# A convolution stem's gradients: paired sums, joins in SBUF, and four more leaves by three products

## The chip, the cores and the metric

The kernel runs on one core of one Trainium2 chip. The metric is the device time in microseconds of one execution; the profile is that of one such execution, and its span runs from the first to the last instruction. TensorE (PE) multiplies matrices into PSUM; VectorE (DVE) and ScalarE (ACT) read PSUM and SBUF; GpSimd (POOL) does small fills; SyncE (SP) issues the transfers.

## What is computed

```python
L = (T - K) // 2 + 1                                   # B, T, D, K = 2, 16000, 256, 31; L = 7985
h = sum over i of einsum('blc,cd->bld', x[:, i:i + 2 * L:2, :], w[i])
mu = mean over l of h;  var = mean over l of (h - mu) ** 2
h = (h - mu) / sqrt(var + 1e-5) * gn_gamma + gn_beta
out = gelu(h)                                          # tanh form
returns out and the gradients of x, w, gn_gamma, gn_beta for grad_out
```

Everything large is bf16. There are three products of the size of the convolution: the forward one, the gradient of x and the gradient of w.

## The kernel before, in words

Each of the three convolutions is cut by three levels of a fast scheme that takes three half-size products in place of four: a sum or difference of operands, called branch or leaf B, and the products A and C. At the outer two levels this gives nine combinations of branch (`br`) and leaf (`lf`). At the innermost level a leaf is done either by four products (`f_leaf`, `g_leaf`, `w_leaf`) or by three: a first part on differenced weights (`f_three_b`, `g_three_b`, `w_pairs`), whose result ACT copies within PSUM with the needed signs, and a second part on summed data added on top (`f_three_ac`, `g_three_ac`, `w_single`). PSUM is a ring of four tiles of 128 x 1024 fp32.

The stages follow each other on PE:

- **Forward** (matmuls at L655): two batches, four chunks each, three branches each. `f_sums` (L609 to 640, its `tt` at L620) makes the summed data: `second` the leaves' operands, `third` the third level's. The leaves of the branches in `FO` are done by three products through `f_outer`, which computes the first parts of A and C into one PSUM tile and copies them with both signs to SBUF (L725); `f_seed` (L735, L739, L792) then adds the B leaf, `RB` and those copies into PSUM ahead of the second parts. `f_evac` (L770, L783) copies the results to SBUF with sums for the mean, and squares them for the variance into a junk tile `JK`.
- **Gelu** (`gelu_unit`, L1014 to L1040) of batch 0 runs beside the forward part of batch 1, that of batch 1 beside the first chunks of the input gradient. A unit is one half of the channels, 128 x 1024: load, Identity and Square on ACT, L1018 on DVE, two sigmoids on ACT (L1020, L1022), L1024 and five products or sums at L1028 on DVE, then two accumulated sums (L1038 on ACT, L1040 on DVE). Its tiles come in rings: three or two sets of h, y and s, and two or one of the scratch tiles y2 and z.
- **Input gradient** (matmuls at L1217): `e_load` and `e_comp` form the gradient of the normalised value, `e_spread` (L1155) lays it out, `g_sums` (L1181) makes the sums. `plain` serves the first three chunks of batch 0, `split` (all leaves by three products) the other five; the results are joined by `g_join` (L1259) and stored. `d2_piece` (L1410) makes differences of the output gradient for the next stage. `w2_outer` makes the differenced weights that `split` needs ahead of the fourth chunk.
- **Weight gradient** (matmuls at L1500): nine combinations in turn. `x_tile` loads x and, in some, adds (`w_add`, L1466); `pair_x` (L1560), `pair_d` (L1568) and `leaf_d` (L1638) make operands. `NODES` lists the ten of eighteen leaves done by three products. The partial sums are fp32 in SBUF; DVE adds them to PSUM (`ve` at L735, `w_both` at L1592) and, at the end of a leaf, writes the output (`w_emit`, L1529).

The order is not the order of the program text. Every operation is recorded by `Plan.add` with a planned duration and the tiles it reads and writes; `Plan.listing` then puts each engine's operations into a fixed list by due times, which the matmuls set, shifted by kind in the table `lead`. The engines run these lists in order. GpSimd's and SP's lists are made in the same way, and all large transfers are issued by SP.

## Time and profile before

| | |
|---|---|
| three runs | 1184.16, 1186.21, 1187.15 us; median 1186.21 |
| the profiled execution | 1185.89 us, span 1184.1 us, mean granted TensorE clock 0.986 |
| PE, weight loads, DVE, ACT busy | 1120.7, 751.0, 1043.5, 595.9 us |
| forward, first to last matmul | 7.9 to 429.5 us |
| input gradient | 429.5 to 862.6 us |
| weight gradient | 862.7 to 1179.0 us |
| transfers | 255 MB, mean 215 GB/s |

Busy time is the time in which at least one instruction of the engine runs; matmuls overlap each other, so their mean duration is longer than their spacing, and neighbouring DVE and ACT instructions overlap a little. In a row of a group stand the line, the engine, the operation with tiles and shapes and the count; then busy time and mean ns of one; then idle time of the engine just ahead of them and what ended it. In a row of the timeline stand start and duration. A window's row gives stretch, length, busy time and count of PE, weight loads, DVE, ACT and POOL, the granted clock, the share of the transfer engines and GB/s.

### The profile page before, as it was taken

The page shows a single profiled execution, that of the slowest core. Times are in us where ns is not written, and L with a number is a line of the kernel's source. Part 1 is how long each engine was busy: PE and PEld are TensorE (multiplying, and loading weights), DVE is VectorE, ACT ScalarE, POOL GpSimd, SP SyncE. Part 2 cuts the span into 40 slices and gives each one's busy share as a digit, 9 for nine tenths or more (in the row PEclk, how much of TensorE's full clock was granted, in tenths as well). Part 3 has the DMA queues.
Part 4 walks back from the last instruction along what each step waited for, and adds up shares of the span by engine and source line. Part 5 has one row for each costly group of instructions (what it writes and reads, how often), then busy time and mean ns, then how long its engine had stood idle before and what let it go on. Part 6 is the DMA issues. An engine that isn't in the chain of part 4 may idle for free.

```text
span 1184.1 us, 19217 instructions
## 1 busy us (share of the span) xinstructions
PE 1120.7 (95%) x7615; PEld 751.0 (63%) x7668; DVE 1043.5 (88%) x1410; ACT 595.9 (50%) x919; POOL 38.7 (3%) x67
## 2 busy tenths in 40 slices
PE   3999999999999969989999899999999999989998
PEld 3888899867677954434444344444478766656785
DVE  6997887899999978989899898889999999689994
ACT  1253444778686488676867777664522202111200
POOL 0000000000000000020000120000000000000000
PEclk7999999999999989999999999999999999999999
DMA  8358658878794798877744999889898717996783
GB/s 213 52 133 154 135 146 179 215 146 207 170 208 124 276 253 270 247 223 196 209 135 126 317 338 300 230 257 296 286 290 295 225 78 240 329 338 204 243 239 99
DMA packets 348334, 255.16 MB, mean 215 GB/s; under 512 B 187734, under 2 KB 328916, under 8 KB 341972
## 3 DMA queue, kind: packets, MB, share of 16 engines
q1 hardware_dynamic: 348052, 253.93, 75.9%
q8 instruction: 60, 0.98, 0.3%
q14 instruction: 30, 0.25, 0.1%
q0 software_dynamic: 192, 0.00, 0.0%
HBM read 118.95 MB, written 89.62 MB: 176 GB/s over the span
## 4 chain that ended last, share of the span: by engine, by line
PE 73%; DVE 10%; DMA 7%; ACT 5%; issue 3%; SPq 1%; POOL 1%; DVEq 0%; POOLq 0%; ACTq 0%; another core or an unknown queue 0%
PE ps L655 34%; PE ps L1500 20%; PE ps L1217 19%; DVE arena L1466 2%; DMA arena<-dnd 2%; DMA d2d<-arena 2%; DVE arena L1410 1%; DMA arena<-in_x_dram 1%; DVE arena L1259 1%; DMA arena<-hd 1%; SPq L480 1%; POOL arena L1146 1%; DVE arena L1181 1%; DMA arena<-d2d 1%; DVE arena L1568 1%
## 5 line engine op out<-in xcount | busy, mean ns | idle before, releaser
L1217 PE MATMUL ps<-arena 128*128 128x512 bf16 (+1 forms) x1834 | 404.5, 380 | 28.9 <-DVE arena L1181 9.0
L655 PE MATMUL ps<-arena 128*128 128x256 bf16 (+4 forms) x3460 | 406.6, 281 | 22.8 <-DVE arena L610 8.7
L655 PEld LDWEIGHTS <-arena 128*128 128x128 bf16 x3460 | 338.4, 99 | 90.8 <-DVE arena L610 8.8
L1217 PEld LDWEIGHTS <-arena 128*128 128x128 bf16 x1872 | 184.3, 99 | 248.8 <-issue 28.7
L1500 PE MATMUL ps<-arena 128*128 128x256 bf16 (+1 forms) x2321 | 309.8, 295 | 6.5 <-DVE arena L1560 4.9
L1500 PEld LDWEIGHTS <-arena 128*128 128x128 bf16 x2336 | 228.3, 98 | 88.0 <-DVE arena L1560 5.7
L750 ACT ACTIVATE arena<-ps 128x1024 bf16<-128x1024 f32 (+1 forms) x129 | 130.8, 1020 | 216.8 <-PE ps L1500 94.5
L620 DVE TENSOR_TENSOR arena<-arena 128x1088 bf16<-128x1088 bf16 (+3 forms) x211 | 174.7, 868 | 18.7 <-PE ps L655 18.1
L1028 DVE TENSOR_TENSOR arena<-arena 128x1024 bf16<-128x1024 bf16 x160 | 107.7, 686 | 10.6 <-ACT arena L1020 7.0
L1181 DVE TENSOR_TENSOR arena<-arena 128x516 bf16<-128x516 bf16 (+3 forms) x212 | 98.2, 495 | 5.3 <-PE ps L1217 2.9
L1466 DVE TENSOR_TENSOR arena<-arena 128x4096 bf16<-128x4096 bf16 x38 | 86.0, 2284 | 3.2 <-PE ps L1500 1.7
L1244 ACT ACTIVATE ps<-ps 128x512 f32<-128x512 f32 x108 | 62.3, 583 | 38.7 <-PE ps L1217 38.7
L1410 DVE TENSOR_TENSOR arena<-arena 128x768 bf16<-128x768 bf16 (+3 forms) x112 | 66.4, 638 | 10.4 <-DMA d2d<-arena 5.7
L770 ACT ACTIVATE arena<-ps 128x512 bf16<-128x512 f32 (+1 forms) x64 | 37.1, 583 | 56.0 <-PE ps L655 55.9
L1259 DVE TENSOR_TENSOR arena<-arena 128x1024 bf16<-128x1024 bf16 x80 | 54.8, 686 | 7.1 <-ACT arena L750 6.8
L1584 ACT COPY ps<-ps 128x256 f32<-128x256 f32 x54 | 19.4, 358 | 76.7 <-PE ps L1500 75.5
L1259 DVE TENSOR_TENSOR arena<-ps,arena 128x1024 bf16<-128x1024 f32 x44 | 53.7, 1220 | 3.4 <-PE ps L1217 3.3
L610 DVE TENSOR_TENSOR arena<-arena 128x2048 bf16<-128x2048 bf16 (+1 forms) x55 | 53.6, 1005 | 0.0
L725 ACT ACTIVATE arena<-ps 128x512 bf16<-128x512 f32 x56 | 29.1, 601 | 46.9 <-PE ps L655 41.7
L1018 DVE SCALAR_TENSOR_TENSOR arena<-arena 128x1024 bf16<-128x1024 bf16 x32 | 39.0, 1221 | 13.1 <-ACT arena L1016 13.0
L1568 DVE TENSOR_TENSOR arena<-arena 128x1024 bf16<-128x1024 bf16 x76 | 48.5, 685 | 1.6 <-DMA arena<-d2d 1.6
L1638 DVE TENSOR_TENSOR arena<-arena 128x2304 bf16<-128x2304 bf16 x36 | 47.7, 1351 | 2.1 <-DMA arena<-d2d 2.1
(77 smaller groups left out, 683.8 us busy)
## 6 DMA issues: line engine op xcount, KB each, us to landing
arena<-in_x_dram SPq DMA_DIRECT2D x40, 1024.0 KB, 9.5
arena<-d2d SPq DMA_DIRECT2D x16, 1216.0 KB, 13.4
out_dram<-arena SPq DMA_DIRECT2D x35, 512.0 KB, 5.6
d2d<-arena SPq DMA_DIRECT2D x30, 384.0 KB, 7.3
arena<-dnd SPq DMA_DIRECT2D x10, 960.0 KB, 5.9
vl<-arena SPq DMA_DIRECT2D x36, 256.0 KB, 3.7
arena<-vl SPq DMA_DIRECT2D x9, 1024.0 KB, 7.6
hd<-arena SPq DMA_DIRECT2D x8, 1024.0 KB, 5.0
```

Source lines behind the costliest of these rows:

```text
L620: lambda: nc.vector.tensor_tensor(out=o, in0=a, in1=b, op=ALU.add))
L655: yield nc.tensor.matmul(ps[:, dh, cs], lhsT=wt, rhs=mv, start=s0, stop=False, skip_group_check=True)
L750: lambda: nc.scalar.activation(out=out, in_=ps, func=ACT.Copy, scale=scale))
L1028: add("DVE", dve(1024), [o], [a, b_], lambda: V.tensor_tensor(out=o, in0=a, in1=b_, op=op))
L1181: lambda: nc.vector.tensor_tensor(out=o, in0=a, in1=b, op=ALU.add))
L1217: yield nc.tensor.matmul(ps[:, e, 0:wide], lhsT=lt, rhs=mv, start=s0, stop=False, skip_group_check=True)
L1244: lambda: nc.scalar.activation(out=ps[:, 1], in_=ps[:, 0], func=ACT.Copy, scale=-1.0))
L1259: add("DVE", dve(1024, rate), [o], [a, b], lambda: nc.vector.tensor_tensor(out=o, in0=a, in1=b, op=op))
L1410: lambda: nc.vector.tensor_tensor(out=out, in0=a, in1=b_, op=ALU.subtract))
L1466: add("DVE", dve(4096), [o], [a, b], lambda: nc.vector.tensor_tensor(out=o, in0=a, in1=b, op=ALU.add))
L1500: yield nc.tensor.matmul(ps[:, s, c0:c1], lhsT=lt, rhs=mv, start=s0, stop=False, skip_group_check=True)
L1568: add("DVE", dve(1024), [d4[:, j]], [d], lambda j=j, o=o, st_=st_: nc.vector.tensor_tensor(out=d4[:, j], in0=d[:, o:o + 3 * st_ + 1:st_, : ...
```

## The change

- Two helpers make access patterns: `cross` reads the two halves of a pair in reverse order, with the second one an element later (a negative step), and `fan` repeats a view twice at a given step (zero or negative too). With them `f_sums`, `g_sums`, `d2_piece` and `pair_d` write both halves of a pair by one instruction in place of two.
- `gelu_unit` works on both channel halves: tiles of 128 x 2048, two sets of h, y and s, one of y2 and z, one of the gradient and output tiles. For batch 1 the six set tiles lie at 94208 to 118784, where `w2_outer` writes later.
- Forward: `f_outer` and the seeding of PSUM in its branches go. `split` gives each leaf its own PSUM tile, does both parts in it, copies the B leaf to `TX` and forms `TP`, its sum or difference with `RB`, in SBUF; `f_evac` copies a leaf to SBUF and joins it there with `TP`. `FV` takes the place of `FO` and adds branch B of chunks 0 to 2 of batch 1.
- Input gradient: `split` makes both joined tiles at once (`VP`), with one `VX` in place of three `VT`, and joins branch B's pair at once.
- Weight gradient: fourteen of eighteen leaves by three products. `w_both` and the seeds in PSUM go: the shared part of a combination is kept in SBUF (`PM`), each finished leaf is copied by ACT and summed in bf16 in SBUF by `w_sum`. `pc_d`, a buffer in DRAM, becomes bf16.
- The table `lead` has new numbers and finer stages.

```diff
+    def cross(v, d):
+        ap = [list(x) for x in v.ap]
+        s, n = ap[d]
+        assert n == 2
+        ap[d] = [1 - s, 2]
+        return bass.AP(tensor=v.tensor, offset=v.offset + s, ap=ap)
+
+    def fan(v, d, s):
+        ap = [list(x) for x in v.ap]
+        ap.insert(d, [s, 2])
+        return bass.AP(tensor=v.tensor, offset=v.offset, ap=ap)
...
+    U = [sb(o, 2, F) for o in (138240, 142592, REG + 14336)]
...
-                tt(E1[:, 0], xt[:, 0, 3], xt[:, 1, 0])
-                tt(E1[:, 1, 0:F - 1], xt[:, 1, 3, 0:F - 1], xt[:, 0, 0, 1:F])
+                tt(E1[:, :, 0:F - 1], xt[:, :, 3, 0:F - 1], cross(xt[:, :, 0, 0:F - 1], 1))
...
-            tt(u[0], o[:, 0], o[:, 1])
-            tt(u[1][:, 0:F - 1], o[:, 1, 0:F - 1], o[:, 0, 1:F])
+            tt(u[:, :, 0:F - 1], o[:, :, 0:F - 1], cross(o[:, :, 0:F - 1], 1))
...
-                tt(lc[:, 0], E1[:, 0], E0[:, 1])
-                tt(lc[:, 1, 0:F - 1], E1[:, 1, 0:F - 1], E0[:, 0, 1:F])
+                tt(lc[:, :, 0:F - 1], E1[:, :, 0:F - 1], cross(E0[:, :, 0:F - 1], 1))
...
-    def f_outer(pt, br, ops, co, we, wd, ts):
...
-            keep(RB[:, 0 if lf == A else 1], flat2(ps))
+            keep(RB[:, 0 if lf == A else 1], flat2(ps), 1.0 if lf == A else -1.0)
+            if t is not None and lf == C_:
+                f_join(RB, RB, fan(t, 1, 0), ALU.add)
...
+        if t is not None:
+            op = ALU.add if lf == A else ALU.subtract
+            v = t[:, 0 if lf == A else 1].rearrange("p (d e f) -> p d e f", d=2, e=2)
+            o = hs[:, :, :, k, 0:wd]
+            f_join(o, o, v[:, :, :, 0:wd], op)
...
+    def f_join(o, a, b, op):
+        add("DVE", dve(o.free_size()), [o], [a, b], lambda: nc.vector.tensor_tensor(out=o, in0=a, in1=b, op=op))
...
-        if outer and br != B_:
-            for lf, j in ((C_, 1), (A, 0)):
-                t = ts[lf].rearrange("p d f -> p (d f)")
-                add("DVE", dve(1024), [t], [RB[:, j], t], lambda t=t, j=j: nc.vector.tensor_tensor(
-                    out=t, in0=RB[:, j], in1=t, op=ALU.add if br == A else ALU.subtract))
...
-    FO = {(0, c, br) for c in range(NCK) for br in ORDER if c or br != B_} | {(1, 3, br) for br in FLAST}
+    FV = {(0, c, br) for c in range(NCK) for br in ORDER if c or br != B_} | {(1, 3, br) for br in ORDER} | {(1, c, B_) for c in range(NCK)}
...
+        def split(b, c, br, sums, co, we, wo):
+            ops, third, second = sums
+            x = free.pop(0)
+            u = {B_: slot(3 - b)}
+            third(B_, u[B_])
+            f_three_b(ring[x], br, B_, ops[B_], co, we)
+            second(A)
+            step()
+            i = {A: free.pop(0)}
+            f_three_b(ring[i[A]], br, A, ops[A], co, we)
+            u[A] = slot(3 - b)
+            third(A, u[A])
+            f_three_ac(ring[x], br, B_, u[B_], co, we, wo)
+            second(C_)
+            keep(TX, flat2(ring[x]))
+            free.append(x)
+            step()
+            if br != B_:
+                f_join(TP, fan(TX, 1, 0), RB, ALU.add if br == A else ALU.subtract)
+            i[C_] = free.pop(0)
+            f_three_b(ring[i[C_]], br, C_, ops[C_], co, we)
+            u[C_] = slot(3 - b)
+            third(C_, u[C_])
+
+            def last(lf):
+                f_three_ac(ring[i[lf]], br, lf, u[lf], co, we, wo)
+                f_evac(b, c, br, lf, ring[i[lf]], TX if br == B_ else TP)
+                free.append(i[lf])
+            last(A)
+            rest.append(lambda: last(C_))
...
-    def gelu_batch(b, base, nset, nscr, ngt, noo, base0, pace):
...
+    def gelu_batch(b, areas, nset, nscr, ngt, noo, base0, pace):
...
+        hs_, ys_, ss_ = (take(nset, 2, 4, HM) for _ in range(3))
+        y2s, zs = (take(nscr, 2, 4, HM) for _ in range(2))
+        gts = take(ngt, 4, 2, XM)
+        oos = take(noo, 8, D) if noo else [None]
...
+        add("DVE", dve(2048, 1), [z], [y2, y],
...
+        add("ACT", act(2048), [s], [z],
...
-                tt(sc[:, :, 1, 0, 0:n], et[:, :, 3, 0, 0:n], et[:, :, 0, 1, 0:n])
-                tt(sc[:, :, 1, 1, 0:n - 1], et[:, :, 3, 1, 0:n - 1], et[:, :, 0, 0, 1:n])
+                tt(sc[:, :, 1, :, 0:n], et[:, :, 3, :, 0:n], cross(et[:, :, 0, :, 0:n], 2))
...
-            tt(u[:, 0, :, 0:n], e[:, :, 0, 0:n], e[:, :, 1, 0:n])
-            tt(u[:, 1, :, 0:n - 1], e[:, :, 1, 0:n - 1], e[:, :, 0, 1:n])
+            tt(u.rearrange("p j d f -> p d j f")[:, :, :, 0:n], e[:, :, :, 0:n], cross(e[:, :, :, 0:n], 2))
...
-                g_join(ts[C_], vx, GRB[:, pr, 1], ALU.subtract if br == A else ALU.add, 2)
-                g_join(vx, vx, GRB[:, pr, 0], ALU.add if br == A else ALU.subtract, 2)
+                ts = {A: VP[:, 0], C_: VP[:, 1]}
+                g_join(VP, fan(VX, 1, 0), GRB[:, pr], ALU.add if br == A else ALU.subtract, 2)
...
+                if br == B_:
+                    keep(GRB[:, pr, j], ps[:], -1.0 if lf == C_ else 1.0)
+                    if lf == C_:
+                        g_join(GRB[:, pr], GRB[:, pr], fan(VX, 1, 0), ALU.subtract, 2)
...
+        sub(t[:, :, 0:n1, :], fan(d0(2 * b1 + 1, n1), 1, -2 * D), fan(d0(2 * b1, n1), 1, 0), [t[:, :, 0:n1, :]], [dt])
...
+            sub(t2[:, k % 2, :, 0:g, :], fan(r1(1), 1, -2 * step * D), fan(r1(0), 1, 0), [t2[:, k % 2]], [v])
...
-    NODES = {(0, A), (0, C_), (1, A), (1, C_), (3, A), (4, A), (6, A), (7, A), (7, C_), (8, C_)}
...
+    NODES = {(n, lf) for n in range(9) for lf in (A, C_)} - {(1, C_), (3, C_), (5, C_), (6, C_)}
...
+    def w_sum(o, a, b):
+        add("DVE", dve(1024), [o], [a, b], lambda: nc.vector.tensor_tensor(out=o, in0=a, in1=b, op=ALU.add))
...
+        last = i1 != A and i2 != B_
+        o = (PE_[0] if n in (2, 5, 6) else w_wo() if last else PB[r3, h] if i2 == B_ else PS[r2, r3, h])
+        keep(o, flat2(ps))
+        if m is not None:
+            w_sum(o, o, m)
+        if n == 2:
+            for k in range(2):
+                w_sum(PS[k, r3, h], PS[k, r3, h], o)
...
+            w_sum(o, o, PB[r3, h])
+            w = o if i1 == C_ else w_wo()
+            w_sum(w, o, PS[r2, r3, h])
+            w_out(w, h, int(i1 == C_), r2, r3)
...
-        for j, o in ((0, o0), (1, o1)):
-            st_ = abs(o0 - o1)
-            add("DVE", dve(1024), [d4[:, j]], [d], lambda j=j, o=o, st_=st_: nc.vector.tensor_tensor(
-                out=d4[:, j], in0=d[:, o:o + 3 * st_ + 1:st_, :], in1=d[:, om:om + 3 * st_ + 1:st_, :], op=ALU.subtract))
+        s = abs(o0 - o1)
+        add("DVE", dve(2048), [d4], [d], lambda: nc.vector.tensor_tensor(
+            out=d4, in0=fan(d[:, o0:o0 + 3 * s + 1:s, :], 1, (o1 - o0) * D), in1=fan(d[:, om:om + 3 * s + 1:s, :], 1, 0), op=ALU.subtract))
...
-    def w_both(ps, t):
...
-                        if seeded:
-                            ve(t, flat2(X[h]), p2[r3, h], ALU.add)
...
+                if pa or pc:
+                    keep(PM[h], flat2(X[h]))
+                if not pa:
+                    keep(flat2(Y[h]), flat2(X[h]))
...
-    RINGS = ((3, 2, 2, 2), (2, 1, 1, 0))
+    RINGS = ((((REG, REG + 41216),), 2, 1, 1, 1), (((94208, 118784), (GREG, GREG + 20992)), 2, 1, 1, 0))
```

More of the change, by code (lines that the diff above doesn't have):

```diff
@@ new lines, in __init__ @@
+            "F1z keep split": -70.0,
+            "F1z load f_evac": -1.5,
+            "F1z tt f_sums": -56.5,
+            "F1z tt second": -16.0,
+            "F1z tt third": -8.5,
+            "F1z turn x_load": -3.5,
+            "F1z w_sub f_again": 22.0,
+            "F1z zero f_evac": -48.5,
+            "F1z zero x_load": -75.0,
+            "G0 cp e_spread": -65.0,
+            "G0 e_comp conv_stem_kernel": 2.0,
+            "G0 g_join last": -0.5,
+            "G0 g_mm g_leaf": -11.5,
@@ new lines, in __init__ @@
+            "G1 zero e_comp": -117.0,
+            "G1 zero e_spread": -14.0,
+            "G1z g_join last": -4.0,
+            "G1z g_join split": 11.0,
+            "G1z g_mm g_three_ac": -285.0,
+            "G1z g_mm g_three_b": 1.5,
+            "G1z g_three_b split": -99.0,
+            "G1z keep last": -46.5,
+            "G1z keep split": -33.5,
+            "G1z load g_store": -43.0,
+            "G1z tt first": -32.0,
+            "G1z tt second": -118.5,
+            "G1z tt third": -40.0,
@@ L189, in __init__ @@
+            "Wz turn out0_late": 24.0,
+            "Wz w_add weight_grad": 2.5,
+            "Wz w_mm w_pairs": -14.5,
+            "Wz w_mm w_single": -136.5,
+            "Wz w_pairs weight_grad": -27.0,
+            "Wz w_sum w_done": -23.5,
         }
@@ L623, in f_sums @@
         else:
[L624 removed]
+            s = S
             E0, E1 = s[:, :, 0], s[:, :, 1]
```

733 lines of the change are left out of this document (348 added, 385 removed).

## The prediction

> **What bounds the kernel now.** I read the page first: busy shares, the forty slices, the chain that ended last.
>
> ```profile
> span 1184.1 us, 19217 instructions
> PE 1120.7 (95%) x7615; PEld 751.0 (63%) x7668; DVE 1043.5 (88%) x1410; ACT 595.9 (50%) x919; POOL 38.7 (3%) x67
> PE 73%; DVE 10%; DMA 7%; ACT 5%; issue 3%; SPq 1%; POOL 1%; DVEq 0%; POOLq 0%; ACTq 0%; another core or an unknown queue 0%
> ```
>
> TensorE (PE) is busy nearly always and carries the chain; VectorE (DVE) is close behind it. The profiled execution took 1185.9 us, 1.8 more than its span and 0.3 less than the median of the three runs (1186.2). Next the view of windows, cut where the matmul line changes (L655 forward, L1217 input gradient, L1500 weight gradient), at 212, where forward turns to batch 1, and at 613, where three chunks of the input gradient end.
>
> ```profile
> 25.50:212.00 186.50, 185.19 (x1691) 165.92 (x1691) 155.70 (x191) 77.12 (x180) 1.86 (x3) 0.99 0.62 131
> 212.00:429.50 217.50, 213.77 (x1708) 166.52 (x1707) 203.36 (x299) 158.03 (x264) 3.33 (x10) 1.00 0.80 194
> 429.50:613.00 183.50, 169.05 (x771) 77.36 (x786) 163.77 (x257) 137.03 (x167) 13.95 (x25) 0.97 0.76 226
> 613.00:862.60 249.60, 235.22 (x1065) 106.87 (x1085) 224.60 (x402) 165.53 (x216) 17.23 (x19) 0.99 0.85 266
> 862.60:1178.80 316.20, 309.68 (x2323) 228.18 (x2335) 278.37 (x242) 53.63 (x88) 0.53 (x1) 1.00 0.75 235
> ```
>
> Each row has the stretch, its length, then busy time of PE, weight loads, DVE and ACT. Forward and weight gradient are PE streams with 1 to 2% of gaps; the input gradient loses 29 us of 433 to waits. So a removed matmul shortens forward and weight gradient by its own time, and VectorE time counts only where PE waits for it.
>
> **Matmuls.** A leaf by four products is, in forward, 16 matmuls of 512 columns and 32 of 256; by three it is 48 of 256. In the weight gradient it is 64 of 512 against 96 of 256.
>
> ```profile
> L1500 PE MATMUL ps<-arena 128*128 128x256 bf16 x1824 | 202.3, 273 | 5.7 <-DVE arena L1560 4.9 <-DVE ps L1592 0.8
> L1500 PE MATMUL ps<-arena 128*128 128x512 bf16 x497 | 111.7, 379 | 0.8
> L1500 PEld LDWEIGHTS <-arena 128*128 128x128 bf16 x2336 | 228.3, 98 | 88.0 <-DVE arena L1560 5.7 <-issue 1.0
> 525.85 139.86 PE L1217 MATMUL ps<-arena 128*128 128x512 bf16 x643 [0.18 <-ACT ps L1244]
> ```
>
> One of 256 costs 202.3/1824 = 0.111 us. One of 512 costs 0.2175 in the unbroken input-gradient run (139.86/643) and 0.218 to 0.225 in the weight gradient (512 issued, 497 recorded); I take 0.22. NODES grows from 10 to 14 of 18 leaves: 4 x (64 x 0.22 - 96 x 0.111) = **-14** us. FV adds branch B of chunks 0 to 2 of batch 1, six leaves: 6 x (16 x 0.22 - 16 x 0.111) = **-10.5**. The input gradient keeps its matmuls.
>
> [...]
>
> **Vector instructions.** Is one double instruction cheaper, and what is a PSUM operand worth? Groups by shape, then three rows of the timeline:
>
> ```profile
> L620 DVE TENSOR_TENSOR arena<-arena 128x1087 bf16<-128x1087 bf16 x85 | 61.0, 723 | 11.9 <-PE ps L655 11.6
> L620 DVE TENSOR_TENSOR arena<-arena 128x2176 bf16<-128x2176 bf16 x31 | 39.7, 1285 | 0.1
> L1181 DVE TENSOR_TENSOR arena<-arena 128x516 bf16<-128x516 bf16 x86 | 35.3, 422 | 0.3 <-PE ps L1217 0.2
> L1181 DVE TENSOR_TENSOR arena<-arena 128x1036 bf16<-128x1036 bf16 x32 | 22.2, 693 | 2.7 <-PE ps L1217 1.6 <-ACT arena L1155 1.1
> L735 DVE TENSOR_TENSOR ps<-ps,arena 128x1024 f32<-128x1024 f32 x28 | 34.2, 1226 | 5.5 <-PE ps L1500 5.5
> L1568 DVE TENSOR_TENSOR arena<-arena 128x1024 bf16<-128x1024 bf16 x76 | 48.5, 685 | 1.6 <-DMA arena<-d2d 1.6
> L1592 DVE TENSOR_TENSOR ps<-ps,arena 128x1024 f32<-128x1024 f32 x20 | 24.2, 1228 | 11.8 <-PE ps L1500 11.7
> 418.42 2.35 DVE L1130 TENSOR_TENSOR arena<-arena 128x2048 bf16<-128x2048 bf16 x2
> 420.69 1.29 DVE L792 TENSOR_TENSOR arena<-arena 128x1024 bf16<-128x1024 bf16 x2
> 421.90 1.23 DVE L739 SCALAR_TENSOR_TENSOR ps<-ps,arena 128x1024 f32<-128x1024 f32 x1
> ```
>
> Two of 1024 take 421.90 - 420.69 = 1.21 us from start to start, one of 2048 takes (420.69 - 418.42)/2 = 1.135. Merging two saves 0.07, not the 0.15 that durations suggest, for neighbours overlap by 0.084. A PSUM operand costs 1226 against 686 ns.
>
> The program holds 1412 Vector instructions before and 1025 after. By these start-to-start prices and the row of each shape, the whole stream falls from 1028 to 984 us (the page's busy time is 1043): forward to the first input-gradient sum 368 to 351, input gradient up to the last gelu reduction 178 to 156, from there to the first sum of the weight gradient 182 to 185, weight gradient 300 to 292. The savings are 28 PSUM seeds and 20 SBUF joins of forward for 39 joins in SBUF (-13), 60 PSUM sums of the weight gradient for 68 `w_sum` (68 x 0.60 against 60 x 1.14: -27, of which the four added leaves' pairs take back 15), and merging. These 44 us hide under PE except at waits.
>
> **The backward operand.** `cross` and `fan` walk their outer dimension with a negative or zero step; inner rows stay contiguous bf16. No DVE row before has a negative step. The zero step occurs (L1592 broadcasts rows of PSUM: 1228 against 1226 for L735), at the slower rate. Bounds: nothing, by the pair rows of L1568, which already hop between rows; or the L735 rate, 0.52 ns more per element. I take nothing: both chains read the same inner rows. [...]
>
> **Scalar work.** ACT gains 102 copies of 256 in `f_three_b`, 84 in `w_pairs` and 34 `keep`, and loses 56 copies of `f_outer`: about +50 us on an engine that is half idle. A `w_pairs` group now waits for three copies (L691 below, about 0.27 apart), while 16 matmuls of the other half (1.8 us) run: covered; without that cover, 1 us a group. In forward another leaf's products, 3 to 5 us, stand between a `f_three_b` and its second part. In exchange PE no longer waits for `w_both`. SP issues 490 transfers in place of 530 (gelu's are twice as large, `pc_d` half as large); no PE wait of the two PE-bound stages ends at a transfer behind the first 20 us, so this is 0.
>
> **The turn from forward to input gradient.** PE waits 9 us here (timeline; then groups, for the prices):
>
> ```profile
> 429.52 0.81 PE L1217 MATMUL ps<-arena 128*128 128x512 bf16 x3
> 440.76 6.49 PE L1217 MATMUL ps<-arena 128*128 128x512 bf16 x20 [9.00 <-DVE arena L1181]
> 439.14 1.22 DVE L1018 SCALAR_TENSOR_TENSOR arena<-arena 128x1024 bf16<-128x1024 bf16 x1 [2.37 <-ACT arena L1016]
> 440.28 0.42 DVE L1181 TENSOR_TENSOR arena<-arena 128x516 bf16<-128x516 bf16 x1
> 433.16 1.05 ACT L783 ACTIVATE arena<-arena 128x1024 bf16<-128x1024 bf16 x1
> ...
> L691 ACT ACTIVATE ps<-ps 128x256 f32<-128x256 f32 x75 | 27.7, 369 | 35.8 <-PE ps L655 34.3
> L770 ACT ACTIVATE arena<-ps 128x460 bf16<-128x460 f32 x16 | 8.8, 552 | 9.9 <-PE ps L655 9.8
> L1155 ACT COPY arena<-arena 128x768 bf16<-128x768 bf16 x32 | 25.2, 828 | 9.1 <-POOL arena L1146 9.1
> L1155 ACT COPY arena<-arena 128x512 bf16<-128x512 bf16 x16 | 9.5, 612 | 0.1
> ```
>
> The sum that PE needs writes over the junk tile of L783 (free at 434.3), but stands behind a gelu operation that waits for ACT. In the new order ten such sums stand ahead of that operation. But the last leaf's join now comes between its copy and the squares, and the `e_spread` copies stand behind the last copies: two copies of the leaf 1.3, two squares 2.3, four spreads of 0.73 and two of 0.51 (ACT neighbours overlap by 0.1), together 7.6, so the first matmul waits that long, then eight matmuls and a copy: 10 us to the three-product part, against 11.3 now. **-1**.
>
> **Gelu in pairs.** `y2` and `z` exist once per pair, so pairs follow each other. One round, by these groups and the first and last start of L1018 and L1040, shapes doubled:
>
> ```profile
> L1016 ACT ACTIVATE arena<-arena,stats 128x1024 bf16<-128x1024 bf16 x32 | 39.5, 1233 | 0.4
> L1020 ACT ACTIVATE arena<-arena 128x1024 bf16<-128x1024 bf16 x32 | 33.7, 1053 | 17.3 <-DVE arena L1018 17.2
> L1018 DVE SCALAR_TENSOR_TENSOR arena<-arena x32: 1215/1219/1227, 229.6 to 620.8; 128x1024 bf16<-128x1024 bf16 x32
> L1040 DVE CUSTOM_DVE_ANT_0 arena<-arena x32: 1215/1219/1227, 240.1 to 629.1; 128x1024 bf16<-128x1024 bf16 x32
> ```
>
> Squares 2.5, L1018 2.3, two sigmoids 3.8, four products 4.9, two sums 2.5: 16 us, 16.5 with hand-overs. Batch 1 starts at 439 and ends at 630, 24 us a pair; now its tiles lie where `w2_outer` writes, so it should end with chunk 2: 3 x 264 matmuls x 0.2175 = 172 us, 21.5 a pair. That fits by 5 us a pair: cost 0, and the later stretch (613 to 862) gains some of the waits around the start of batch 1: **-3**, between 0 and -13.
>
> **Weight-gradient supply.**
>
> ```profile
> L1466 DVE TENSOR_TENSOR arena<-arena 128x4096 bf16<-128x4096 bf16 x38 | 86.0, 2284 | 3.2 <-PE ps L1500 1.7 <-DMA arena<-in_x_dram 1.5
> L1638 DVE TENSOR_TENSOR arena<-arena 128x2304 bf16<-128x2304 bf16 x36 | 47.7, 1351 | 2.1 <-DMA arena<-d2d 2.1
> L750 ACT ACTIVATE arena<-ps 128x1024 bf16<-128x1024 f32 x96 | 97.1, 1019 | 61.4 <-PE ps L1217 39.5 <-PE ps L655 19.3 <-DVE arena L1410 2.0
> L1529 DVE TENSOR_TENSOR arena<-ps,arena 128x512 bf16<-128x512 f32 x1 | 0.7, 692 | 4.0 <-PE ps L1500 4.0
> ```
>
> DVE needs 292 us beside PE's 302 (316 - 14), unevenly. Combination 2, with both leaves now by three products: six `w_add` 13.2 (four of them the next x tiles), twelve pair instructions 13.6, four `leaf_d` 5.1, twelve `w_sum` 7.2, together 39 us of DVE in 288 x 0.111 = 32 of PE. Combination 1 loses one such leaf and gives reserve, so I add **+3** (0 to 8) of waits.
>
> **The end.** The last output now takes a `keep` (1.02, L750) and three sums (3 x 0.6) where L1529 took one of 0.7; less overlap, **+2.5** (1 to 3).
>
> Sum: 1185.9 - 14 - 10.5 - 1 - 3 + 3 + 2.5 = **1163 us**.
>
> **Rivals.**
> (a) *The waits go too.* Less DVE work also clears most of the 29 us that the input gradient loses; against it: ACT and DMA end as many of these waits. 13 more: 1150.
> (b) *Gelu misses its new end.* If the pairs keep today's 24 us, batch 1 ends 21 us after chunk 2 and PE stands: 1163 + 21 = 1184, no change. For it: in-order queues at 90%; against: before had time until 630.
> [...]
> (d) *Three products save nothing*, since their weight loads are not hidden: in the weight gradient 96 x (0.098 + 0.111) = 20.1 us against 64 x (0.098 + 0.22) = 20.4. 1163 + 24.5 = 1187. [...]
>
> **How the numbers follow.** Forecast 0.60 (its own range 1153 to 1174, from the bounds above); (a) 0.12; (b) 0.10; (c) 0.08; (d) 0.03; 0.07 for part of (b) with more supply waits, 1175 to 1182. About 0.3% (3.6 us) is what a measurement of this kernel can tell from no change: faster holds the forecast, (a), the remainder and part of (b), 0.83; same 0.09; slower 0.08. Range 1149 to 1180.
>
> **What would show it.** Weight gradient near 305 us from first to last matmul, batch 1's forward near 207; merged sums at 1.28 us for 2174 elements and 0.69 for 1032 (1.2 at 1032 would mean (c)); last gelu reduction no later than the third chunk's end and no PE gap over 5 us there (else (b)); 256-column matmuls still at 0.111 (else (d)). The forecast is wrong if forward or weight gradient shows PE gaps of more than 10 us that are not there now.

## The result, and the profile after

The changed kernel takes 1156.1 us (median of 4 runs, 1155.0 to 1157.9) where before takes 1186.0 beside it: a ratio of 0.975, interval 0.973 to 0.977. In a later run of the same kernel (e9 below) it came to 0.972 (0.970 to 0.975). The forecast was 1163, the range 1149 to 1180. The profiled execution took 1.8 us beyond its span.

The page of the changed kernel, busy shares and chain:

```profile
span 1154.5 us, 19110 instructions
PE 1097.9 (95%) x7750; PEld 762.9 (66%) x7796; DVE 1000.6 (87%) x1023; ACT 660.0 (57%) x1045; POOL 23.5 (2%) x67
PE 26%; DMA 8%; DVE 7%; ACT 2%; issue 2%; SPq 1%; POOL 0%; DVEq 0%; ACTq 0%; POOLq 0%
```

TensorE is still 95% busy: the span lost 29.6 us and TensorE's busy time 22.8. The shares of this chain add up to 46% only (before's to 100%), so the rest of the reading goes by stretches. The view of windows, cut at the turn of the batches in forward (207.6, after 1706 wide matmuls; before's 212 comes after 1707), at the last forward matmul, the first of the input gradient, 613 and the start of the weight gradient:

```profile
20.22:207.60 187.38, 187.38 (x1706) 167.99 (x1707) 145.32 (x134) 89.43 (x215) 1.92 (x3) 1.00 0.64 134
207.60:424.50 216.90, 205.64 (x1709) 166.21 (x1706) 198.54 (x209) 159.54 (x264) 3.74 (x11) 1.00 0.80 203
424.50:432.50 8.00, 0.09 (x2) 0.19 (x3) 4.44 (x11) 7.82 (x15) 0.00 (x0) 0.73 0.67 192
432.50:613.00 180.50, 179.66 (x827) 82.83 (x843) 169.86 (x202) 140.08 (x156) 6.73 (x20) 0.99 0.79 224
613.00:847.00 234.00, 223.59 (x1010) 101.40 (x1030) 198.20 (x221) 154.23 (x200) 8.80 (x23) 0.99 0.92 278
847.00:1148.50 301.50, 297.19 (x2457) 240.44 (x2463) 270.65 (x230) 104.33 (x192) 0.53 (x1) 1.00 0.76 237
```

As in the prediction, a row has the stretch, its length, then the busy time of PE, weight loads, DVE, ACT and POOL. Batch 1's forward lost 8 us of matmuls and hardly any length; the input gradient lost waits and no matmuls; the weight gradient lost both. From these cuts and the waits that the timeline of PE shows:

| stretch | before: length (waits of PE) | after | forecast | measured |
|---|---|---|---|---|
| start to the first wide matmul | 20.6 | 20.2 | 0 | -0.4 |
| forward | 408.8 (6.3) | 404.3 (11.1) | -10.5 | -4.5 |
| last forward matmul to last of the input gradient | 433.4 (26.9) | 422.6 (17.0) | -4 | -10.8 |
| weight gradient | 316.1 (5.7) | 301.4 (3.7) | -11 | -14.7 |
| behind the last matmul | 5.1 | 6.0 | +2.5 | +0.9 |
| sum | 1184.1 | 1154.5 | -23 | -29.6 |

The new waits of forward, in the timeline of PE (start, length, then the idle time ahead of the row and what ended it):

```profile
214.74 16.82 PE L741 MATMUL ps<-arena 128*128 128x256 bf16 x152 [0.39 <-ACT arena L827]
232.88 25.46 PE L741 MATMUL ps<-arena 128*128 128x512 bf16 x184 [1.32 <-DVE ps L801]
259.08 15.04 PE L741 MATMUL ps<-arena 128*128 128x256 bf16 x120 [0.74 <-DVE arena L709]
275.76 8.05 PE L741 MATMUL ps<-arena 128*128 128x256 bf16 x72 [1.64 <-ACT arena L805]
284.65 16.13 PE L741 MATMUL ps<-arena 128*128 128x256 bf16 x128 [0.84 <-ACT arena L805]
...
347.31 27.38 PE L741 MATMUL ps<-arena 128*128 128x512 bf16 x204 [1.36 <-DVE ps L801]
```

Twelve waits of 0.3 to 1.6 us in batch 1, each for a copy, a seed, a sum or a difference of weights that another engine had not yet done; before had two there:

```profile
265.91 56.90 PE L655 MATMUL ps<-arena 128*128 128x256 bf16 x424 [1.85 <-ACT ps L691]
324.66 104.81 PE L655 MATMUL ps<-arena 128*128 128x256 bf16 x884 [1.85 <-ACT ps L691]
```

The groups by shape that the prediction named as signs:

```profile
L709 DVE TENSOR_TENSOR arena<-arena 128x2174 bf16<-128x2174 bf16 x91 | 116.4, 1290 | 42.6 <-PE ps L741 42.0
L709 DVE TENSOR_TENSOR arena<-arena 128x2176 bf16<-128x2176 bf16 x31 | 39.8, 1285 | 1.1 <-DVE arena L856 0.9
L1271 DVE TENSOR_TENSOR arena<-arena 128x1032 bf16<-128x1032 bf16 x86 | 58.5, 692 | 7.4 <-PE ps L1304 5.6 <-ACT arena L1245 1.1 <-remote 0.5
L1271 DVE TENSOR_TENSOR arena<-arena 128x1036 bf16<-128x1036 bf16 x32 | 22.0, 691 | 2.7 <-PE ps L1304 2.6
L1583 PE MATMUL ps<-arena 128*128 128x256 bf16 x2208 | 243.1, 273 | 3.9 <-DVE arena L1641 1.2 <-DVE arena L1346 1.2 <-DMA arena<-d2d 0.7
```

The groups of 2174 and 1032 elements have the backward operand, those of 2176 and 1036 have none, and with it an instruction costs as much as without: 1290 ns against 1285, 692 against 691. 256-column matmuls stay at 243.1/2208 = 0.110 us. The last gelu reduction, in the timeline of VectorE:

```profile
598.58 1.22 DVE L1130 CUSTOM_DVE_ANT_0 arena<-arena 128x1024 bf16<-128x1024 bf16 x1
```

It ends at 599.8, before at 630; TensorE shows no wait from 432.5 to 651.7.

### The profile page after: what moved, and what is told of

The parts are those of the page before. It is cut to its first block, busy times and chain, and to the rows that moved or that the text cites. A ratio compares the mean times of both kernels' runs of the same rounds, so it can differ in the third digit from the quotient of the medians.

```text
span 1154.5 us, 19110 instructions
## 1 busy us (share of the span) xinstructions
PE 1097.9 (95%) x7750; PEld 762.9 (66%) x7796; DVE 1000.6 (87%) x1023; ACT 660.0 (57%) x1045; POOL 23.5 (2%) x67
## 5 line engine op out<-in xcount | busy, mean ns | idle before, releaser
L805 ACT ACTIVATE arena<-ps 128x1024 bf16<-128x1024 f32 (+1 forms) x168 | 170.6, 1020 | 237.3 <-PE ps L1583 131.6
L1583 PE MATMUL ps<-arena 128*128 128x256 bf16 (+1 forms) x2456 | 297.3, 283 | 4.3 <-DVE arena L1641 1.2
L709 DVE TENSOR_TENSOR arena<-arena 128x2174 bf16<-128x2174 bf16 (+2 forms) x132 | 175.5, 1349 | 43.7 <-PE ps L741 42.0
L1114 DVE TENSOR_TENSOR arena<-arena 128x2048 bf16<-128x2048 bf16 x80 | 97.5, 1219 | 14.2 <-ACT arena L1106 9.1
L1271 DVE TENSOR_TENSOR arena<-arena 128x1032 bf16<-128x1032 bf16 (+2 forms) x126 | 88.8, 726 | 10.1 <-PE ps L1304 8.1
L777 ACT ACTIVATE ps<-ps 128x256 f32<-128x256 f32 x177 | 63.7, 369 | 47.4 <-PE ps L741 44.1
L1331 ACT ACTIVATE ps<-ps 128x512 f32<-128x512 f32 x108 | 62.6, 584 | 43.8 <-PE ps L1304 41.3
L1662 ACT COPY ps<-ps 128x256 f32<-128x256 f32 x138 | 49.3, 357 | 51.0 <-PE ps L1583 48.1
L1102 ACT ACTIVATE arena<-arena,stats 128x1024 bf16<-128x1024 bf16 x64 | 76.2, 1230 | 1.3 <-DMA arena<-hd 1.0
L827 ACT ACTIVATE arena<-ps 128x512 bf16<-128x512 f32 (+1 forms) x64 | 37.0, 582 | 59.9 <-PE ps L741 59.8
L1493 DVE TENSOR_TENSOR arena<-arena 128x1536 bf16<-128x1536 bf16 (+3 forms) x56 | 62.0, 1124 | 9.8 <-DMA d2d<-arena 5.9
L1601 DVE TENSOR_TENSOR arena<-arena 128x1024 bf16<-128x1024 bf16 x68 | 45.5, 685 | 21.5 <-ACT arena L805 21.1
L1346 DVE TENSOR_TENSOR arena<-arena 128x2048 bf16<-128x2048 bf16 (+1 forms) x50 | 50.3, 1006 | 13.2 <-ACT arena L805 13.0
L1346 DVE TENSOR_TENSOR arena<-ps,arena 128x1024 bf16<-128x1024 f32 x44 | 53.4, 1217 | 3.5 <-PE ps L1304 2.3
L1648 DVE TENSOR_TENSOR arena<-arena 128x2048 bf16<-128x2048 bf16 x46 | 54.7, 1217 | 0.2
L1641 DVE TENSOR_TENSOR arena<-arena 128x2048 bf16<-128x2048 bf16 x46 | 54.8, 1216 | 0.0
```

The costliest lines, as they stand in the source:

```text
L709: lambda: nc.vector.tensor_tensor(out=o, in0=a, in1=b, op=ALU.add))
L777: lambda o=o, i=i, sc=sc: nc.scalar.activation(out=o, in_=i, func=ACT.Copy, scale=sc))
L805: lambda: nc.scalar.activation(out=out, in_=ps, func=ACT.Copy, scale=scale))
L1102: lambda o=o, func=func, i=h[:, dh], sc=sc, bi=bi: SC.activation(out=o, in_=i, func=func, bias=bi, scale=sc))
L1114: add("DVE", dve(2048), [o], [a, b_], lambda: V.tensor_tensor(out=o, in0=a, in1=b_, op=op))
L1271: lambda: nc.vector.tensor_tensor(out=o, in0=a, in1=b, op=ALU.add))
```

## The experiments

Left open by the traces: whether the matmuls made the gain as priced, what made forward's new waits, and why the input gradient lost 9.9 us of waits where only a few were forecast. The rival theories: VectorE's shorter stream took the waits away; the doubled instructions did; or neither, and it is the order in which the planner lists the same work, which the new table of offsets (`lead`) sets.

**e1, ten leaves.** The four added leaves of the weight gradient taken back:

```diff
-    NODES = {(n, lf) for n in range(9) for lf in (A, C_)} - {(1, C_), (3, C_), (5, C_), (6, C_)}
+    NODES = {(0, A), (0, C_), (1, A), (1, C_), (3, A), (4, A), (6, A), (7, A), (7, C_), (8, C_)}
```

> The changed kernel with the ten leaves of before by three products in place of fourteen; the whole result is still computed. My theory: four leaves cost 64 x 0.22 - 96 x 0.111 = 3.5 us each more on TensorE, which is the bound of the weight gradient, so its matmuls take 301.6 + 14 = 316 us from first to last and the kernel 1170 us; VectorE has some 15 us less to do there and nothing comes of that. Rival 1: three products save nothing, because the weight loads are not hidden: 1156, unchanged. Rival 2: the four leaves were paid for with waits at VectorE (the changed kernel still has 3.7 us of gaps in this stage): then those go as well, and the kernel takes 1166.

Measured: 1210.0 us, 1.019 of before (1.017 to 1.021). All three theories miss it by 40 us or more. Forward, whose instructions are as in the changed kernel, took the same 404.4 us; from there on the planner had listed everything anew. Waits of PE, then the stretch from the first matmul of the weight gradient to behind the last:

```profile
PE ps L1304 <- ACT arena L805: 13.3, 5, 9.6
...
PE ps L1583 <- DVE arena L1709: 7.9, 1, 7.9
...
PE ps L1583 <- DVE arena L1641: 5.2, 1, 5.2
```

```profile
858.50:1202.50 344.00, 318.96 (x2350) 232.14 (x2347) 256.19 (x211) 99.97 (x173) 0.53 (x1) 0.97 0.67 214
```

One wait for a PSUM copy in the input gradient is 9.6 us long, and the weight gradient begins with waits of 5.2 and 7.9 for VectorE, although VectorE has less to do in it (256 us against 271). Of the 319 us of PE, 14 records (3 us) are late ones of the input gradient; 316 remain, at a granted clock of 0.97. The same matmuls took 309.7 in before at a clock of 1.00, and the changed kernel's 297.2: the four leaves are worth 12.5, and the other 6 go with the lower clock. So the matmuls that went shorten TensorE's time, and rival 1 falls; rival 2 stays open, for the time of this kernel says nothing on it: a change to the set of operations is also a change of the order.

**e2, branch B by four products.**

```diff
-    FV = {(0, c, br) for c in range(NCK) for br in ORDER if c or br != B_} | {(1, 3, br) for br in ORDER} | {(1, c, B_) for c in range(NCK)}
+    FV = {(0, c, br) for c in range(NCK) for br in ORDER if c or br != B_} | {(1, 3, br) for br in ORDER}
```

> The changed kernel with branch B of chunks 0 to 2 of batch 1 by four products again, as before; the whole result is still computed. The forward of the changed kernel came out only 4.5 us shorter, not 10.5, and has 11.1 us of gaps in batch 1 where before had some 5. Theory A: the six leaves do save 6 x 16 x 0.109 = 10.5 us, and the gaps come from gelu instructions of double length that stand ahead of PSUM copies in the queues of ScalarE and VectorE: the gaps stay near 11 us and the kernel takes 1156 + 10.5 = 1166.5. Theory B: the gaps come with the three products themselves (copies by a factor of -1 and the copy of the first PSUM result, which four products do without): the gaps fall to 6 us and the kernel takes 1162.

Measured: 1185.9 us, 0.9986 of before (0.9973 to 0.9999). Forward 423.6 us instead of 404.3, with TensorE busy 13 us longer and 17.6 us of waits, 14.9 of them in batch 1; the weight gradient, untouched by the edit, 307.3 instead of 301.4. Theory B's gaps of 6 did not come, but since the order changed here too this doesn't decide between A and B.

**e3 and e4, single sums and gelu halves, as the planner lists them.** e3 writes each `cross` sum and each `pair_d` as two; e4 puts gelu's sums and sigmoids in a loop over `dh`:

```diff
-            tt(u[:, :, 0:F - 1], o[:, :, 0:F - 1], cross(o[:, :, 0:F - 1], 1))
+            tt(u[:, 0], o[:, 0], o[:, 1])
+            tt(u[:, 1, 0:F - 1], o[:, 1, 0:F - 1], o[:, 0, 1:F])
...
-        tt(y, y, s, ALU.mult)
+        for dh in range(2):
+            yy, vv, zz, ss = y[:, dh], y2[:, dh], z[:, dh], s[:, dh]
...
+            tt(yy, yy, ss, ALU.mult)
```

> The changed kernel with every sum that has a backward operand, and the pair differences of the weight gradient, issued as two instructions again: 91 + 86 + 46 instructions become twice as many; same results. My theory: 0.07 us each, 16 us of VectorE time, 6.4 in forward, 6 in the input gradient, 3.2 in the weight gradient, nearly all beside TensorE's work: 1156 to 1159. Rival: the waits that the input gradient lost (26.6 us of gaps behind the start of its three-product part before and 9 now, and forward's short waits at VectorE) hang on VectorE's shorter stream: then the time comes back, 1156 + 6 + 3 = 1165 or more. By either, the halves show 0.72 us at 1087 elements and 0.42 at 516, so that a backward operand costs nothing when two halves at 1.44 - 0.08 stand against 1.29 for the whole.

> The changed kernel with seven VectorE instructions and two sigmoids of a gelu pair issued per channel half again (1024 elements in place of 2048); tiles, loads and results as in the changed kernel. Theory A: instructions of double length, up to 2.3 us, hold back PSUM copies that TensorE waits for in batch 1's forward; with halves the gaps there fall from 11 to 6 us: 1151. Theory B: the double instructions save VectorE 16 x 7 x 0.07 = 8 us and ScalarE 3 us, half of that in each batch, and the input gradient's waits went because of it: 1160 to 1164, with more gaps between 432 and 613 us. Theory C: neither, both engines have room: 1156.

Measured: e3 1224.6 us (1.031, 1.028 to 1.033), e4 1221.0 us (1.028, 1.026 to 1.030). No theory had either. In e3 the three longest waits of PE behind the start are 10.8 us for a difference of weights (`w_sub`) in the input gradient, 7.1 for an input transfer in the weight gradient and 5.6 for a `leaf_d`, none of which the edit touched. The fourth, 5.5 us in forward, does end at the half of a split sum (L709, 1088 elements), so the order and the halves can't be told apart here. So from here on the edits keep the order: the planner sees the changed kernel's operations, and only what an operation issues is changed.

**e5, two sums in one place.**

```diff
+    def both(o, a, b, d):
+        k = (slice(None),) * d
+        for i in range(2):
+            yield nc.vector.tensor_tensor(out=o[k + (i,)], in0=a[k + (i,)], in1=b[k + (i,)], op=ALU.add)
...
-                lambda: nc.vector.tensor_tensor(out=o, in0=a, in1=b, op=ALU.add))
+                lambda: both(o, a, b, d) if d else nc.vector.tensor_tensor(out=o, in0=a, in1=b, op=ALU.add))
```

> As e3, with the order of the changed kernel kept on every engine: the planner still sees one sum, and the sum is issued as two instructions, one behind the other, at its place (91 in forward, 86 in the input gradient, 46 in the weight gradient); same results. e3 lost 64 us, most of it in waits that moved with the planner's order. Theory A: merging is worth its 0.07 us each on VectorE and nothing on the path, since 15 us more are hidden beside TensorE: 1156 to 1158. Theory B: the waits that the input gradient lost (8.5 us) were bought by the shorter VectorE stream: 1162 to 1165. Theory C, that e3's 64 us are the price of the sums themselves and not of the order: above 1200.

Measured: 1154.1 us, 0.972 of before (0.970 to 0.974). The page of e5, and its groups by shape:

```profile
PE 1095.7 (95%) x7750; PEld 762.6 (66%) x7796; DVE 1015.6 (88%) x1246; ACT 660.6 (57%) x1045; POOL 24.6 (2%) x67
```

```profile
L579 DVE TENSOR_TENSOR arena<-arena 128x1087 bf16<-128x1087 bf16 x182 | 124.1, 722 | 32.6 <-PE ps L746 30.5 <-issue 1.6
L579 DVE TENSOR_TENSOR arena<-arena 128x516 bf16<-128x516 bf16 x172 | 64.3, 420 | 4.4 <-PE ps L1309 3.0 <-ACT arena L1250 1.1
```

L579 is `both`. VectorE issues 223 instructions more and is busy 15.2 us longer than in e9, 0.068 each, and none of it reaches the time: the waits of the input gradient are 7.9 and 7.7 us, as in e9 (7.9 and 8.3). Theory A's mechanism holds (its 1156 to 1158 lies 2 us too high, and the changed kernel's own runs in e9 spread from 1151.6 to 1156.2), B and C fall: issued in the kept order the halves cost nothing that can be measured, so nearly all of e3's 68 us came with the order.

**e6, gelu halves in one place.** As e5, for the seven VectorE instructions and the two sigmoids of a pair:

```diff
-            add("DVE", dve(2048), [o], [a, b_], lambda: V.tensor_tensor(out=o, in0=a, in1=b_, op=op))
+            add("DVE", dve(2048), [o], [a, b_], lambda: (V.tensor_tensor(
+                out=o[:, i], in0=a[:, i], in1=b_[:, i], op=op) for i in range(2)))
```

> As e4, with the order of the changed kernel kept: each double gelu instruction is issued as two halves, one behind the other, at its place; same results. VectorE gets 16 x 7 x 0.07 = 8 us more, ScalarE 32 x 0.1 = 3 us. Theory A (both engines have room, the order makes e4's loss): 1156 to 1158. Theory B (gelu decides the input gradient's waits and VectorE's load): 1160 to 1164, with gaps at 432 to 613 us. Theory C (e4's 64 us are the price of the halves): above 1200.

Measured: 1153.2 us (0.972, 0.970 to 0.974), VectorE 1006.0 us busy (e9: 1000.4), the input gradient's waits 7.9 and 7.8, those of batch 1's forward 10.5 us (e9: 11.1). Theory A again; as an instruction, the doubling of gelu is worth nothing here. Its tiles, which belong to the pair, were not undone.

**e7, half of batch 0's gelu left out.** From the third pair of batch 0 on, e6's loops run over the first half alone, so the second half's output and gradient aren't computed:

```diff
+        hs = range(1 if b == 0 and 2 * c + e > 1 else 2)
...
+                out=o[:, i], in0=a[:, i], in1=b_[:, i], op=op) for i in hs))
```

> The changed kernel, order kept, but fourteen instruction places of gelu's work in batch 0 left out by half: from the third pair on, the nine double instructions of a pair treat the first channel half alone, so that the second half of gelu's output and gradient in batch 0 is not computed. It takes long instructions out of the queues while TensorE works on batch 1's forward, and leaves the three-product leaves as they are. Theory A: the 11 us of short gaps in batch 1's forward come from gelu instructions of up to 2.3 us ahead of PSUM copies: gaps 3 to 5 us, 1149 to 1151. Theory B: they come with the three products of branch B: gaps stay at 10 to 11, 1155 to 1156.

Measured: 1151.6 us (0.970, 0.968 to 0.972). Forward 399.9 us where e9 has 403.3, with 7.9 us of waits in batch 1 where e9 has 11.1. Neither theory's gaps came: some 3 of the 11 us hang on the gelu work that stands in the queues, the larger part doesn't. That the length of one instruction matters is not shown: e6, with halves at the same places and all of the work, kept 10.5. Two of the waits that stay, in the timeline of PE:

```profile
232.28 25.46 PE L741 MATMUL ps<-arena 128*128 128x512 bf16 x184 [1.32 <-DVE ps L801]
...
274.67 9.80 PE L741 MATMUL ps<-arena 128*128 128x256 bf16 x88 [1.65 <-ACT arena L805]
```

These are the seed of a four-product leaf and the copy of the first result (`keep(TX)`) of a three-product leaf, at the places of the changed kernel: there TensorE had nothing else listed between.

**e8, the turn.** The six spread copies of the first chunk on VectorE, at the place of the first:

```diff
+            if (b, c) == (0, 0):
+                k = len(late)
+                late.append((o, i))
+                add("ACT", act(n), [o], [i], lambda k=k: (nc.vector.tensor_copy(out=o, in_=i) for o, i in (() if k else late)))
```

> The changed kernel, order kept, with the six copies that spread the first chunk of the input gradient (ScalarE, at the turn from forward) issued on VectorE, at the place of the first of them; same results. TensorE waits there from 424.5 to 432.4 us. My theory: the copies stand on ScalarE between and behind two squares of the last forward leaf, and VectorE is idle in 427.7 to 430.1; they are done by 428.5 in place of 432.0, and the first matmul starts at 429 and the three-product part some 3.5 us earlier: 1152.6. Rival: VectorE's sum for the second part stands behind the statistics, which wait for the squares, so TensorE gets a second wait: 1155. Rival 2: the order behind it moves so that another wait takes the place: 1156.

Measured: 1153.7 us (0.972, 0.970 to 0.973), no difference from e9 that the intervals show. The timeline of PE at the turn:

```profile
428.15 2.86 PE L1310 MATMUL ps<-arena 128*128 128x512 bf16 x7 [4.23 <-issue]
433.63 6.59 PE L1310 MATMUL ps<-arena 128*128 128x512 bf16 x22 [2.62 <-DVE arena L1277]
```

The wait of 7.9 us became 4.2 and 2.6, together 6.9: the first rival, though the sum waited for another reason. The sum that PE waits for (L1277) began at 432.7, when a store of forward's output (`hd`) had read the tile that the sum's result overlaps; the copies stand ahead of forward's last join, which ends 4.3 us behind the last forward matmul instead of 2.0.

**e9, the changed kernel again**, and **e10, the turn with another tile**:

> The changed kernel unaltered, as the measure for e5 to e8 and the next run: e5, e6 and e8 came out 2 to 3 us under its 1156.1 with matmul runs of the same count 0.2% shorter (193.2 to 193.7 us for 1768 matmuls against 194.1). If that was the run of the chip, this gives 1153 to 1155 here; if their edits gave it, 1156.

Measured: 1155.7 us (0.972, 0.970 to 0.975): e5, e6 and e8 don't differ from it by more than the intervals allow. Its page:

```profile
PE 1096.9 (95%) x7750; PEld 762.4 (66%) x7796; DVE 1000.4 (87%) x1023; ACT 660.1 (57%) x1045; POOL 22.9 (2%) x67
```

```diff
+        def head():
+            for f in late if b else ():
+                yield f()
+            yield V.tensor_reduce(out=s1, in_=hsum[b][:], axis=AX.X, op=ALU.add)
...
+            if (k, lf) == (0, B_):
+                w = GU[0][A]
+                late.append(lambda: nc.vector.tensor_tensor(out=w.rearrange("p j d f -> p d j f")[:, :, :, 0:n],
+                                                            in0=e[:, :, :, 0:n], in1=cross(e[:, :, :, 0:n], 2), op=ALU.add))
...
+                return
```

> The changed kernel, order kept but for the turn from forward to input gradient: the six spread copies on VectorE as in e8, now behind the last forward join and ahead of the statistics, and the first sum for the three-product part behind them, in a tile that does not overlap the forward output still being stored (in e8 this sum waited for that store until 432.7). Same results. My theory: last join 425.8 to 426.5, copies until 429, squares on ScalarE until 428.3, first matmul at 429, three-product part from 431 in place of 434.3: 3.3 us less than e9. Rival: the square root of the statistics (its table load takes 1.28 us) stands ahead of the copy that the three-product part needs, and nothing is gained behind the first eight matmuls: 1 us less than e9.

Measured: 1194.7 us (1.006, 1.005 to 1.008). The order was not kept: the table goes by the names of an operation's function and its caller, and issued from `third` instead of `tt` that one sum lost its offset of 14.5 us. Forward got 18.9 us of waits in batch 1, the weight gradient 16.5, and in the new order the spread copies stand behind the first matmuls that read them, so the start of the input gradient is computed from other contents of the tile. Nothing follows for the turn. But another due time for one operation of 0.7 us was enough to list forward anew, and the kernel took 39 us more than e9.

**e11 and e12, both kernels with an empty table.**

```diff
-        self.lead = {
-            ...
-        }
+        self.lead = {}
```

> The changed kernel with an empty table of due-time offsets, so that its planner orders the work by due times alone; same operations, same results. Theory A (the operations make the gain, the table only keeps them in step): against before with an empty table (e12), 20 to 30 us faster, by the 22 us of matmuls that went and some joins. Theory B (the gain is that of the table): no faster than e12. e1 to e4, where the table met another set of operations, lost 30 to 68 us, so both e11 and e12 may lie 30 to 70 us above their tuned kernels.

> Before with an empty table of due-time offsets; same operations, same results. Its offsets are 0.5 to 30 us where the changed kernel's reach 320, so it should lose less by it: 1200 to 1230. Theory A of e11: 20 to 30 us slower than e11. Theory B: no slower than e11.

Measured: e11 1216.8 us (1.024 of before, 1.022 to 1.026), e12 1228.3 us (1.034, 1.032 to 1.036). Without tables the change is worth 11.5 us, with them 30: neither theory's number, but between the two. Windows of e11, cut as in the table above (forward, to the end of the input gradient, weight gradient), then of e12:

```profile
26.90:451.50 424.60, 390.32 (x3364) 332.82 (x3366) 340.07 (x339) 254.30 (x484) 5.71 (x14) 0.96 0.67 156
451.50:892.50 441.00, 407.90 (x1837) 185.45 (x1873) 372.26 (x430) 298.61 (x365) 17.22 (x43) 0.97 0.82 248
892.50:1209.70 317.20, 302.21 (x2456) 243.30 (x2461) 269.13 (x228) 103.16 (x191) 0.53 (x1) 0.97 0.73 224
```

```profile
26.40:447.80 421.40, 399.30 (x3364) 330.42 (x3364) 351.12 (x474) 233.35 (x444) 5.73 (x14) 0.98 0.65 153
447.80:884.00 436.20, 404.65 (x1834) 184.51 (x1873) 393.12 (x665) 303.26 (x384) 15.90 (x43) 0.97 0.83 248
884.00:1223.60 339.60, 316.05 (x2323) 230.88 (x2335) 282.08 (x243) 54.75 (x89) 0.53 (x1) 0.97 0.71 225
```

The matmuls give what they give with the tables: 9.0 us in forward, 13.8 in the weight gradient. The waits (length less PE's busy time) do not: forward 22.1 to 34.3, the input gradient 31.6 to 33.1, the weight gradient 23.6 to 15.0. With the tables they go 6.3 to 11.1, 26.9 to 17.0 and 5.7 to 3.7. So in both pairs the new operations add waits in forward and take some from the weight gradient; the input gradient loses its waits only between the two tuned orders. Behind its first wait, at the turn (17.4 us in e12, 7.6 in e11), they even rise from 14 to 26 us without tables, although VectorE has 21 us less to do there.

## Why the prediction was right

Its mechanism was: TensorE is the bound, removed matmuls count, VectorE's time does not. TensorE's busy time fell by 22.8 us of the 29.6, so that carried the time. But two stretches erred by 6 to 7 us on opposite sides, forward by +6.0 and the input gradient with the turn by -6.8; that they cancel is luck. The time alone doesn't separate the forecast from rival (a), for 1156.1 lies halfway between 1163 and 1150.

- **Matmuls of the weight gradient, -14.** The mechanism held: PE's time there fell from 310.4 to 297.7, by 12.7. The price of a 512-column matmul was too high. It was read in the input gradient, where before's trace has 1834 of 1872 records, so that 139.86/643 took too many microseconds for one; e1 has all of them:

```profile
432.05 155.52 PE L1304 MATMUL ps<-arena 128*128 128x512 bf16 x724 [7.54 <-issue]
```

  At 155.52/724 = 0.215, and 0.110 for 256 columns, a leaf saves 64 x 0.215 - 96 x 0.110 = 3.2 us, four of them 12.8.
- **Matmuls of forward, -10.5.** PE's busy time in batch 1 fell by 8.1; at 0.215 six leaves make 6 x 16 x 0.105 = 10.1, so some 2 us stay unexplained. Batch 0, with the same matmuls, took 1.4 less at a granted clock of 1.00 instead of 0.98, and lost 2.6 us of waits. Before's row for it:

```profile
20.64:212.00 191.36, 188.78 (x1707) 168.29 (x1708) 160.56 (x194) 78.22 (x182) 1.86 (x3) 0.98 0.63 135
```

  But batch 1 got 7.4 us of new waits, so forward shrank by 4.5 and batch 1's forward took 217, not 207. This is the step that failed: the forecast put no price on waits in forward. Under "**Scalar work**" it weighed only the copies between a `f_three_b` and its second part, and these did not get worse: L777 has 1.8 us of waits where before's L691 had 3.7 in batch 1. The others end, by the profile, at seeds of four-product leaves (L801), copies out of PSUM (L805 `keep`, L827 in `f_evac`), sums (L709) and a difference of weights (1.1 us):

```profile
PE ps L741 <- ACT arena L805: 2.5, 2, 1.6
PE ps L741 <- DVE ps L801: 2.7, 2, 1.4
PE ps L741 <- ACT ps L777: 1.8, 3, 1.1
PE ps L741 <- DVE arena L709: 1.8, 2, 1.1
PE ps L741 <- ACT arena L827: 1.2, 2, 0.8
```

  Some 3 us hang on gelu's work in the queues (e7); what makes the others, the operations or the order, stays open, since e2 changed both. The bound that was set (more than 10 us of new gaps) was not reached.
- **Vector instructions.** Right: 0.07 for a merged pair (0.068 in e5), all of it hidden. VectorE's busy time fell by 42.9 us, forecast 44. (The 540 ns put down to a PSUM operand go with fp32 as well; these rows don't part the two.) Rival (a)'s reason, less VectorE work clears the waits of the input gradient, finds no support, though waits went: e5 and e6 give VectorE 15 and 6 of the 43 us back and no wait returns, and from e12 to e11 its work falls and the waits don't. Giving all of it back in the kept order was not tried.
- **The backward operand at nothing.** Right: 1290 ns for 2174 elements against 1285 for 2176 without it, 692 ns for 1032 against 691 for 1036. Rival (c), which 1.2 us at 1032 elements would have meant, falls.
- **Scalar work hidden.** ScalarE's busy time rose by 64 us, not 50; in the weight gradient, where 84 of the copies came in, 0.2 us of waits end at it. In the input gradient 8.1 of the 9.1 us behind the turn end at its copies out of PSUM (L805), where before had 7.8 at the same copies (L750).
- **The turn, -1.** The wait went from 9.4 to 7.9 us, and it ends, as worked out (7.6), at the spread copies.
- **Gelu in pairs.** Right: batch 1 ended by the end of chunk 2 and rival (b) falls. **The later part, -3** (0 to -13): the waits behind the turn fell from 17.5 to 9.1, inside the bounds. Half of it, 4.2 us, went ahead of 613, where none was forecast to go. The other 4.2 went between 650 and 720, and by the count of matmuls (three chunks of 264, and 216 for each of the other five) the stage turns to batch 1 at some 652, so the place was right. By the profile the waits that went ended at ScalarE's copies in `g_three_b` (L1244 6.3 us, now L1331 0.2) and at joins (L1259 3.4, now L1346 0.8). Whether gelu's earlier end was the reason stays open: the same gelu without tables takes no waits away from the stage (e11, e12), so it needs the tuned order at least. Which entries of the table do it was not tried.
- **Weight gradient supply, +3.** The sign was wrong: waits fell by 2.0, and by 8.6 without tables. VectorE has 271 us in 301 and was not the bound; e1 waited more with less.
- **The end, +2.5.** The copy and three sums came, 3.2 us; but two sums of L1529, not one, had stood there (1.8), and the last store landed 0.5 earlier: +0.9.
- **Rival (d).** Falls: 240 us of weight loads and 297 of matmuls share 301.5 us, as 228 and 310 shared 316 before.

No experiment gave a kernel that can be told from the changed one as faster: e5, e6 and e8 lie at 0.972 like e9, and e7 leaves work out.

## What to carry to other kernels

In a kernel whose order a planner lists, price the bound engine's own instructions from rows whose records are complete, and give the short waits a term of their own with a range, for they hang on the order as much as on the operations. One long wait whose order could be read off was forecast well (the turn, 7.6 against 7.9 us); the many short ones were not. To price one edit, keep the order and change only what an operation issues; an edit that is planned anew tests the planner first (e1 to e4 lost 30 to 68 us, of which the edits' own prices, some 10 to 13 in e1 and e2, are the smaller part).

## What was not expected of the hardware

- The bf16 sums with a negative outer step took 692 ns for 1032 elements (1290 for 2174) where forward ones took 691 for 1036 (1285 for 2176).
- Two halves of an instruction, one behind the other, cost 0.068 us more than the whole (e5: 223 of them, 15.2 us of busy time).
- The granted clock was lower in the executions in which PE waited more: 0.993 over the changed kernel, 0.986 over before, 0.967 in e11. In the weight gradient it was 1.00 where no wait exceeded 3.1 us (before, the changed kernel) and 0.97 where two exceeded 5 (e1, e11); the same matmuls took 302.2 us of PE's time in e11 instead of 297.2. No run was made to show which of the two brings the other.
